# A neighbourhood-attention kernel whose start is re-ordered, whose TensorE runs dummy matmuls at the beginning, and whose first store moves to another queue

## The chip, the cores and the metric

One core of a Trainium2 chip. The metric is the time of the launch in device microseconds (us), taken over several runs; a trace is of one run, and its span is some 2 us shorter than that run's time. A run is called slow when it took over 1.5% longer than the fastest of the same kernel. The "clock" is the share of full speed that PE was granted, as the profile prints it. Engines: PE is TensorE (PEld its weight loads), DVE VectorE, ACT ScalarE, POOL GpSimd, SP the queue of SyncE. "L425" is line 425 of the kernel in question; a line has other numbers in the changed kernel.

## The reference

Dilated neighbourhood attention on a 224 x 224 image with 192 channels, one head, 7 x 7 neighbours at dilation 2, the window clipped at the borders:

```python
H = W = 224; C = 192; ks, dil = 7, 2
q, k, v = split(x @ wqkv)
r0 = clip(arange(H) - 6, 0, H - 1 - 12);  c0 = clip(arange(W) - 6, 0, W - 1 - 12)
ri = r0[:, None] + 2 * arange(7);         ci = c0[:, None] + 2 * arange(7)
logits = einsum(q, k[ri, ci]) * C ** -0.5            # 49 per pixel
o = einsum(softmax(logits), v[ri, ci]) @ wo
```

## The kernel before

Dilation 2 splits the image into even and odd rows and columns. The kernel works in 28 steps, numbered from 0: 14 row blocks j, each with two row classes rc. A step has 8 ticks; a tick takes one column class cc and three or four column tiles n. The query and key weights are folded into products AW, so that a "G" tensor (AW times x) is multiplied with x itself. Masks and one-hot keys ride along as extra rows of the contraction (the tiles called gbt and xb).

```python
for si, st in enumerate(steps):                   # 28 steps
    ...                                           # (cut) lists of work to slip in
    for ti, (cc, ns) in enumerate(st.od):         # 8 ticks
        G = s_stage(st, cc, ns)                   # scores: xa/ga and xb/gbt matmuls, exp on ACT
        if fill: fill.pop(0)()                    # (condition shortened) a G piece, or an output piece of the last step
        if prev is not None:
            y_stage(prev)                         # p (exp of scores) times x rows: needs the xn loads
            ...                                   # y_evac: two evictions, ACT and DVE
        if ti > 0:
            for f in pool_q[:2]: f()              # loads of x rows from POOL, key copies
            n_sp = 4 if st.rc == 0 else 1
            run(sp_q[:n_sp])                      # loads of x rows from SP
        if ti == 1 and st.rc == 0:
            load_xt(st.j + 2)                     # transposed block by DMA, on SP
```

`store` writes a step's output near the end of the following step. A usual step has 5 transfers. The two border steps have each row apart, 16 or so, and before the change all 16 of step 0 went through SP. Before step 0 the start loads 28 pieces of x, turns them on PE (84 transposes), makes the AW products and all of the first G kinds 0 and 1. Step 0's `first_fill` makes the rest, and all five further mask rows:

```python
def f4():
    for gi in range(1, NG):
        mask_row(gi)                              # DVE, 5 of them
    fill_groups(1)
    spread_keys(...); spread_cols(...); spread_rows(nc.sync, 1, NG); ...
    run(k01); run(p11); run(k11)                  # key copies, 7 loads on POOL, key copies
```

The softmax here doesn't subtract the row's maximum and nothing guards it: scores larger than these inputs give would overflow.

## Time and profile before

| | before |
|---|---|
| median time | 373.3 us (371.11 to 375.67, 15 runs) |
| span of the trace | 370.4 us |
| first scores / start of step 1 / step 2 / step 3 | 21.99 / 42.84 / 54.27 / 72.21 us |
| PE busy, share of the span | 336.4 us, 91% |
| PE idle on a DMA at the y matmuls | 6.0 us, 2 times |

Two stretches of 5 us show more:

```profile
35.00:40.00 5.00, 2.49 (x28) 1.83 (x29) 2.37 (x6) 1.68 (x4) 2.90 (x8) 0.58 1.08 207
40.00:45.00 5.00, 5.00 (x56) 3.51 (x54) 1.88 (x4) 3.40 (x8) 4.88 (x12) 0.74 0.60 131
```

After a pause of PE that ends at 37.51 the clock was 0.50 until 42.64, with PE busy for all of these 5.1 us.

### The profile page before, as it was taken

The numbers are of one execution on the slowest core, as the hardware profiler recorded it, in microseconds if no ns is written. First come the engines' busy times: TensorE is split into PE (matmuls) and PEld (weight loads), VectorE is DVE, ScalarE is ACT, GpSimd is POOL, SyncE is SP. The second block draws the span as 40 slices with busy tenths as digits, with TensorE's granted clock in tenths as the row PEclk, the third lists the DMA queues.
The fourth block names the chain that finished last, engine by engine and source line by source line (L and its number), as shares of the span: only waits on it lengthen the run. The fifth ranks groups of instructions, "written<-read, shape, count | busy, mean of one in ns | idle before, by whom it ended". The sixth has DMA issues, their size and how long they took to land.

```text
span 370.4 us, 12803 instructions
## 1 busy us (share of the span) xinstructions
PE 336.4 (91%) x5012; PEld 284.0 (77%) x5012; DVE 276.7 (75%) x692; ACT 238.9 (64%) x540; POOL 237.2 (64%) x481
## 2 busy tenths in 40 slices
PE   5876996799999999999899999999999999999990
PEld 2644685688888888788788888888888888888880
DVE  2779376487877877878787787877778888778791
ACT  4544674467677677776676767677676776677651
POOL 9639737168767697657966778667697649972002
PEclk9999699899999999999999999999999999999996
DMA  5849714676978659579695765957869586553233
GB/s 142 195 97 216 147 22 112 137 183 157 187 205 194 169 156 254 135 105 234 167 238 151 190 179 154 256 128 180 182 162 261 131 195 162 158 128 95 58 96 78
DMA packets 101808, 59.24 MB, mean 160 GB/s; under 512 B 83936, under 2 KB 96232, under 8 KB 101747
## 3 DMA queue, kind: packets, MB, share of 16 engines
q1 hardware_dynamic: 89315, 45.59, 52.7%
q0 software_dynamic: 11888, 12.29, 13.4%
q8 instruction: 39, 0.64, 0.7%
q10 hardware_dynamic: 544, 0.54, 0.6%
q14 instruction: 22, 0.18, 0.2%
HBM read 19.56 MB, written 19.27 MB: 105 GB/s over the span
## 4 chain that ended last, share of the span: by engine, by line
PE 58%; DVE 24%; SPq 5%; ACT 5%; DMA 3%; issue 2%; POOL 0%; POOLq 0%; DVEq 0%
PE pg L341 17%; PE y L425 14%; PE po L443 11%; DVE ysb L439 8%; PE s_ps L397 7%; PE s_ps L398 7%; DVE o_all L456 5%; DVE gbt L347 4%; ACT gbt L348 4%; SPq L504 3%; DMA xn<-in_x_dram 2%; SPq L86 2%; PE pe L307 2%; DVE gbt L236 2%; DVE xb L279 1%
## 5 line engine op out<-in xcount | busy, mean ns | idle before, releaser
L86 POOL DMA_DIRECT2D xn<-in_x_dram x245 | 136.5, 587 | 79.1 <-PE y L425 69.9
L402 ACT ACTIVATE p_sb<-s_ps 128x448 bf16<-128x448 f32 (+1 forms) x224 | 107.2, 490 | 33.4 <-PE s_ps L398 31.7
L425 PE MATMUL y<-p_sb,xn 128*128 128x112 bf16 (+3 forms) x1736 | 113.6, 207 | 6.0 <-DMA xn<-in_x_dram 6.0
L425 PEld LDWEIGHTS <-xn 128*128 128x128 bf16 (+1 forms) x1736 | 98.7, 98 | 23.1 <-DMA xn<-in_x_dram 6.3
L456 DVE TENSOR_TENSOR o_all<-po,rs 128x384 bf16<-128x384 f32 x189 | 105.3, 557 | 8.7 <-DVE rs L455 0.7
L341 PE MATMUL pg<-xt,aw 128*128 128x436 bf16 (+2 forms) x588 | 105.9, 299 | 4.2 <-DVE gbt L348 1.6
L397 PE MATMUL s_ps<-ga,xa 128*128 128x112 bf16 (+3 forms) x812 | 103.3, 211 | 0.6 <-ACT ga L344 0.6
L443 PE MATMUL po<-WP,ysb 128*128 128x193 bf16 x784 | 100.5, 249 | 3.5 <-ACT gbt L348 2.1
L398 PE MATMUL s_ps<-gbt,xb 128*128 128x112 bf16 (+3 forms) x812 | 102.0, 211 | 0.0
L439 DVE CAST ysb<-y 128x448 bf16<-128x448 f32 x104 | 64.6, 622 | 27.7 <-PE y L425 24.5
L397 PEld LDWEIGHTS <-xa 128*128 128x128 bf16 (+1 forms) x812 | 78.1, 99 | 5.4 <-issue 2.1
L398 PEld LDWEIGHTS <-xb 128*128 128x128 bf16 (+1 forms) x812 | 78.2, 99 | 3.5 <-issue 0.6
L443 PEld LDWEIGHTS <-ysb 128*128 128x128 bf16 x784 | 59.3, 98 | 8.6 <-issue 4.0
L439 ACT CAST ysb<-y 128x448 bf16<-128x448 f32 x104 | 57.6, 554 | 6.4 <-PE y L425 6.3
L341 PEld LDWEIGHTS <-aw 128*128 128x128 bf16 x588 | 42.6, 100 | 20.2 <-DVE o_all L456 6.1
L348 ACT CAST gbt<-pg 64x424 bf16<-64x424 f32 x54 | 27.4, 508 | 44.3 <-DVE gbt L347 44.3
L275 POOL COPY xa<-xt 128x896 bf16<-128x896 bf16 x56 | 53.0, 996 | 0.0
L455 DVE RECIPROCAL rs<-po 128x2 f32<-128x2 f32 x189 | 31.0, 164 | 27.5 <-PE po L443 25.6
L344 ACT CAST ga<-pg 128x436 bf16<-128x436 f32 x56 | 29.7, 530 | 26.3 <-PE pg L341 26.3
L347 DVE CAST gbt<-pg 64x436 bf16<-64x436 f32 x54 | 32.4, 599 | 3.9 <-PE pg L341 3.8
L365 POOL COPY ga<-ge 128x24 bf16<-128x24 bf16 (+5 forms) x60 | 20.9, 357 | 15.5 <-DVE ge L315 9.7
L350 ACT CAST ga<-pg 128x424 bf16<-128x424 f32 x56 | 28.7, 512 | 1.3 <-PE pg L341 1.2
(66 smaller groups left out, 152.3 us busy)
## 6 DMA issues: line engine op xcount, KB each, us to landing
out_dram<-o_all SPq DMA_DIRECT2D x26, 630.0 KB
xn<-in_x_dram POOLq DMA_DIRECT2D x245, 48.0 KB, 4.1
xn<-in_x_dram SPq DMA_DIRECT2D x147, 48.0 KB
out_dram<-o_all SPq DMA_DIRECT2D x11, 78.8 KB
gbt<-gbt SPq DMA_DIRECT2D x3, 280.0 KB
out_dram<-o_all SPq DMA_DIRECT2D x52, 9.0 KB
xb<-xb SPq DMA_DIRECT2D x3, 224.0 KB
out_dram<-o_all SPq DMA_DIRECT2D x26, 18.0 KB
```

Source lines behind the costliest of these rows:

```text
L86: eng.dma_start(out=XN[rc][p0:p0 + 64, XP * n + 128:XP * (n + 1)], in_=xp[r0: r0 + 15: 2, TW * n: TW * (n + 1), :])
L275: nc.gpsimd.tensor_copy(out=XA[:, cc, rc, :, q].rearrange("p n (r c) -> p r n c", c=TW), in_=t[:, 2 * cc, rc:16:2, :].rearrange("p r (n c) ...
L341: nc.tensor.matmul(pg[:, a_ - ra:b_ - ra, p0:p0 + S - 3], lhsT=AW[w], rhs=xt[b][:, k, la:lb:2, p0:p0 + S - 3], start=(i == 0), stop=(i == ...
L347: e0(out=Bt[0][0:64, ra:rb, 3:S], in_=pg[0:64, :, 0:S - 3])
L348: e1(out=Bt[1][64:128, ra:rb, 6:S], in_=pg[64:128, :, 3:S - 3])
L397: nc.tensor.matmul(o, lhsT=XA[:, cc, st.rc, n, G.kp], rhs=A[cc][:, :, a:b], start=True, stop=False)
L398: nc.tensor.matmul(o, lhsT=XB[:, cc, st.rc, n, G.kp], rhs=Bt[cc][:, :, a:b], start=False, stop=True)
L402: nc.scalar.activation(out=G.p[G.kp, 0:off], in_=s_ps[G.kp, 0:off], func=ACTF.Exp)
L425: nc.tensor.matmul(ys[kt][:, :, a_ - h0:b_ - h0], lhsT=xn[G.kp, l0:l0 + 128], rhs=pv[:, :, a_ - a:b_ - a], start=not ys[2 + kt], stop=True ...
L439: eng(out=dst, in_=src.rearrange("p r i t -> p t i r"))
L443: nc.tensor.matmul(po, lhsT=st.ysb[cc][:, kt, t, :], rhs=WP[:, cc, kt, :], start=(kt == 0), stop=(kt == 1))
L456: nc.vector.tensor_tensor(out=st.o[:, t], in0=po[:, :, 0:C], in1=rs[:].to_broadcast([128, 2, C]), op=ALU.mult)
```

## The change

The intent is to fill PE's idle places at the start. In four parts:

1. The right half of x (column tiles 7 to 13) is loaded and turned first; scores start as soon as its half of G is there, and the left half is turned inside step 0. 13 of the AW pieces become copies on POOL.
2. Dummy matmuls on zeros are to keep PE's clock up: 12 and 2 before the transposes, one behind each group of seven transposes, one a tick in step 0, four small ones behind each score group of step 0.
3. The border store of step 0 gets an output tile of its own and goes out on POOL, one transfer at the end of a step. In odd steps SP is given two loads a tick, not one.
4. Mask rows 3 to 5 are made in steps 1 to 3 instead of step 0.

The core of the diff (cut: the order of loads, the halves of the key copies and one-hots, the list of what step 0 does in which tick):

```diff
-    run(xn_items(0, 0, nc.sync))
-    run(xn_items(1, 0, nc.gpsimd))
-    load_xt(1)
+    first_n = list(range(NT // 2, NT)) + list(range(NT // 2))
+    x00, x10 = xn_items(0, 0, nc.sync), [xn_items(1, 0, e) for e in (nc.scalar, nc.gpsimd, nc.sync)]
+    run(x10[0][n] for n in first_n[:2]); run(x00[n] for n in first_n); run(x10[2][n] for n in first_n[11:])
+    def warm(n_):
+        t = ps_go.tile([128, 512], F32, name="warm", tag="go")
+        for i in range(n_):
+            nc.tensor.matmul(t[:], lhsT=zero[:, 0:128], rhs=zero[:], start=True, stop=True)
...
+    def edge_weights():                           # 13 pieces
+            nc.gpsimd.tensor_copy(out=AW[dst][...], in_=AW[src][...])
...
+    turn_x(1)                                     # right half; left half: turn_x(0) in step 0
+    late = [g_half(1, 1)]
+    g_half(0, 1)
+    edge_weights()
...
+            if st.border and not last:
+                edge_q.append(lambda dst=dst, src=src: nc.gpsimd.dma_start(out=dst, in_=src))
+        run(edge_q[:1]); del edge_q[:1]           # at the end of each step
...
-                n_sp = 4 if st.rc == 0 else 1
+                n_sp = 4 if st.rc == 0 else 2
...
+            if 0 < si < NG - 2 and ti == 5:
+                mask_row(si + 2)
+                spread_rows(nc.sync, si + 2, si + 3)
```

## The prediction

> **What bounds the kernel now.** I read the page first, for its two PE rows, then the busy time by stretch with the stretches cut at the step starts, then the start-up and two idle places of PE instruction by instruction, and last the queue of SP, because the longest idle place ends on a transfer.
>
> ```profile
> PE 336.4 (91%) x5012; PEld 284.0 (77%) x5012; DVE 276.7 (75%) x692; ACT 238.9 (64%) x540; POOL 237.2 (64%) x481
> PE   5876996799999999999899999999999999999990
> ```
>
> Of 370.4 us PE is busy 336.4. The tenths show where it is not: the first eight or so slices (0 to 70 us) and the last. In between it is full, so nothing in the middle can pay unless it takes PE work away, and this change takes none away.
>
> The kernel has 28 steps with 29 first-half score matmuls (L397) each, so every 29th of them in the trace starts a step: 21.99, 42.84, 54.27, 72.21, 83.50, 95.24, ... The busy time by stretch, cut there (columns: stretch, length, busy us and count of PE, PEld, DVE, ACT, POOL, then PE clock, DMA share, GB/s):
>
> ```profile
> 21.99:42.84 20.85, 17.09 (x178) 11.21 (x178) 14.79 (x26) 9.76 (x26) 16.55 (x32) 0.84 0.93 180
> 42.84:54.27 11.43, 11.22 (x171) 9.62 (x169) 8.36 (x22) 8.25 (x19) 5.18 (x11) 1.00 0.11 25
> 54.27:72.21 17.94, 12.64 (x185) 10.80 (x183) 9.23 (x24) 8.26 (x19) 8.42 (x16) 0.90 0.45 106
> 72.21:83.50 11.29, 11.08 (x173) 9.57 (x171) 9.27 (x23) 8.13 (x19) 8.08 (x16) 1.00 0.81 199
> 291.46:303.20 11.74, 11.50 (x186) 9.92 (x183) 8.99 (x24) 8.15 (x19) 8.43 (x16) 1.00 0.70 170
> ```
>
> Odd steps take 11.3 us and even ones 11.7, with PE 98% busy. Step 0 takes 20.85, step 2 takes 17.94. So there are three sums to win: what lies before 21.99 (no scores yet), the excess of step 0, and 17.94 - 11.69 = 6.25 us in step 2.
>
> The step 2 excess is one wait, seen in PE's and SP's timelines:
>
> ```profile
> 61.79 0.36 PE L425 MATMUL y<-p_sb,xn 128*128 128x112 bf16 x4
> 67.21 0.29 PE L425 MATMUL y<-p_sb,xn 128*128 128x64 bf16 x2 [5.06 <-DMA xn<-in_x_dram]
> ...
> 36.48 3.40 SPq L86 DMA_DIRECT2D xn<-in_x_dram  x5
> 53.80 11.03 SPq L504 DMA_DIRECT2D out_dram<-o_all  x16
> 64.88 3.51 SPq L86 DMA_DIRECT2D xn<-in_x_dram  x5
> ```
>
> SP is given six loads of x rows in step 1. Five go out at 36.48, and the sixth stands behind the store of border step 0, which is 16 small transfers, starts only when the outputs are done (53.8) and holds the queue 11.03 us. The load leaves at 64.88, and PE idles 5.06 us for it. The other 1.2 us is the slow clock after the pause.
>
> Step 0 is long for two reasons, in DVE's and POOL's timelines:
>
> ```profile
> 25.78 5.12 DVE L236 CAST gbt<-rm 32x896 bf16<-32x896 f32 x5
> 30.94 0.70 DVE L262 COPY xn<-grp 128x896 bf16<-128x896 bf16 x2
> 31.63 3.59 DVE L279 COPY xb<-xt 64x896 bf16<-64x896 bf16 x4
> 35.25 1.16 DVE L436 CAST ysb<-y 128x448 bf16<-128x448 f32 x2
> ...
> 29.82 4.15 POOL L86 DMA_DIRECT2D xn<-in_x_dram  x7
> 33.91 2.10 POOL L275 COPY xa<-xt 128x896 bf16<-128x896 bf16 x2
> 35.96 0.82 POOL L298 COPY xe<-xt 128x144 bf16<-128x144 bf16 x2
> ```
>
> DVE is without a gap from 25.8 to 36.9, and the evictions that PE needs (y, then the kind-1 G piece) stand behind five mask rows; PE idles 3.8 us, until 37.51. POOL meanwhile reaches the edge gather of block 1, which PE needs for the next step, at 35.96, too.
>
> **What the Trainium skill says.** "TensorE: Matmul & The Clock Gate", Part 1: The HAM clock gate, has PE at half rate until about 3.4 us of sustained matmuls and again after an idle window. The trace agrees: 128x112 score matmuls start 0.09 us apart at 22 us and 0.05 apart at 26 us, and the clock is 0.90 in the stretch with the 5 us pause. The dummy matmuls of the change are for this. "DMA: Bandwidth & Descriptors", Issuing engines are not separate DMA queues: spreading issues over engines saves only the sequencer's time to initiate. That time is just what counts here: 14 loads hold SP 9.16 us (0.65 each), 16 stores 11.03. "SBUF — State Buffer", Who interferes with whom: DVE copies in a two-port mode and GpSimd lock each other out. The trace fits: the key copy of L279 took 0.38 us at 19.42 and about 1.06 at 33, beside POOL's copies.
>
> **The change, part by part.** (1) Before step 0. Now 28 loads are awaited, all 84 transposes done, and all of the first G made, before scores at 21.99. The change loads and turns the right half first and makes only its half of G kinds 0 and 1. Its right-half loads are 7 on SP (after one weight load: 0.75 + 0.6 + 7 x 0.65 = 5.9), 2 on ACT, 5 on POOL after some 1.7 us of iotas (3.0 + 5 x 0.6 = 6.0). With 3.4 us from issue to landing (the DMA view's median before 16 us) they are in at 9.4. PE first runs 12 dummies of 512 columns: about 0.43 us each at the half rate (0.09 per 112 columns), 5 us or a little less, to 6.5. Then 8 weight transposes, their copies, now on two engines, and the AW products, whose copies drop from 17 to 8 because 13 pieces go later to POOL: to about 9.0. 42 transposes at 0.056 (36 took 2.1 us) plus 6 dummies of 0.21 are 3.7: 12.7. A copy 0.39, six G matmuls 0.6, ACT's eviction of the second G piece 0.5, small gaps: scores at 14.4, that is 7.6 earlier. Masks and one-hots lie beside the loads on an idle DVE.
>
> (2) Step 0. It takes on the left half: 42 transposes with six evictions of 0.39 to 0.53 (15.0 to 19.2), then gathering edges on POOL 0.9, G halves 1.0, the edge product, which must wait for a free PSUM buffer (21.2 to 21.8). The third score group then starts at about 21.8. Its seven followers each add scores 0.4, y 0.4, a dummy 0.2 and their share of G, WP and weight turns, 1.0 to 1.8 a tick: PE alone would reach step 1 at about 33. POOL is later: edges of block 0 are done at 24.4 (2.0 us as now), two half key copies 1.0, seven loads 4.15, two key copies 2.0 to 2.6, two more 2.1, gather 0.85: 34.5 to 35.1. PE runs the block 1 edge product 0.6 and two G pieces 0.9 after that: step 1 at about 36.2 instead of 42.84. That is 6.6 us. Of the 7.6 won at the front, 1.0 is given back. DVE has about 15 us of work in these 22, after three of five mask rows (3.1 us) are moved out.
>
> (3) The border store goes to POOL, one transfer at the end of each of 16 steps, from a tile of its own, and in odd steps SP gets two loads a tick, so all six leave before any store. This removes the wait of step 2 whole: 6.25 us. On POOL, 16 issues of about 0.6 us in steps where it is 74% busy (8.4 of 11.5) should be hidden.
>
> (4) Given back: mask rows of 1.02 us fall into steps 1, 2, 3, where DVE has 2.5 us free per step but evictions stand behind them; I charge 1.0 in all.
>
> Sum: 6.6 + 6.25 - 1.0 = 11.9. 373.2 - 11.9 = 361.3; I say 361.
>
> **The rivals.** A, *the front only moves*: the first scores come early, but step 0 swells to 26 us or more, because transposes, edge weights and key copies are pushed into it, so step 1 starts at 40 to 42 and only the step 2 wait is won. For it: POOL is already 16.55 of 20.85 busy in step 0 and gets 13 more copies (which I put at about 0.2 each from the 0.22 to 0.34 of its small edge copies) before it. Against: those lie mostly before the scores, and the moved mask rows free DVE. Time: 365 to 367. B, *the wait of step 2 is taken over*: the load is on time, but POOL's stores or the late load of block 2 (now issued at the end of step 0, some 6 us of SP) hold up what step 2 needs. For it: SP has about 17 us of issues to make between 15 and 32. Against: the six loads then leave by 42 and are needed at 50. Time: 363 to 366. C, *POOL is not the end of step 0*: its loads and copies start earlier than I have them, and PE's own work sets step 1 at 32 to 33. Time: 357 to 358. D, *all hidden already*: not credible, since the idle is on PE, which is full everywhere else.
>
> **Range and chances.** Rivals C and A give 357 and 367; with the scatter of the runs (371.97 to 375.67) the eight-in-ten range is 356.5 to 366. Faster by over 2% means under 365.8: it needs 7.5 of 11.9 us, and the step 2 wait alone is 6.25, so 0.90; within 2% 0.095; slower 0.005.
>
> **What would show it.** First scores near 14.4 (13.5 to 15.5), step 1 near 36 (33 to 38) with POOL's edge gather of block 1 just ahead of it, step 2 about 11.7 long without a DMA wait at its y matmuls, SP without a run of 16 stores, steps 1 to 3 longer than 11.3 and 11.7 by 1.0 together, steps from 5 on unchanged, half-rate matmuls gone after about 7 us. I am wrong if step 1 starts after 40, if step 2 keeps a wait over 2 us, or if later steps grow because of the stores on POOL.

## The result

The changed kernel takes 362.39 us (361.57 to 363.28, 10 runs) against 373.3. The ratio is 0.9705, 95% interval 0.9682 to 0.9728: 3.0% faster. A ratio here is the mean time of one kernel's fast runs over that of the other's of the same rounds, so not quite the ratio of the medians quoted beside it.

The page of the changed kernel, its first line of engines, the PE row, and the group of y matmuls:

```profile
PE 339.8 (94%) x5084; PEld 284.0 (79%) x5084; DVE 277.3 (77%) x702; ACT 236.4 (66%) x528; POOL 245.8 (68%) x507
...
PE   8999999999999999999999999999999999999980
...
L473 PE MATMUL y<-p_sb,xn 128*128 128x112 bf16 (+3 forms) x1736 | 112.3, 207 | 0.0
```

PE is now full from the second slice on, and in the last line the idle time before y matmuls, 6.0 us before, is 0.0. (Some of the busy time at the start is dummies.) Busy time by stretch, cut at the step starts, as before:

```profile
14.64:38.24 23.60, 22.15 (x276) 14.05 (x276) 15.79 (x35) 12.31 (x29) 13.80 (x30) 1.00 0.73 166
38.24:50.25 12.01, 11.51 (x171) 9.72 (x169) 8.70 (x22) 8.34 (x19) 8.76 (x19) 1.00 0.84 145
50.25:61.94 11.69, 11.45 (x185) 9.86 (x183) 9.94 (x27) 8.16 (x19) 9.59 (x18) 1.00 0.93 129
...
73.51:85.87 12.36, 11.63 (x186) 9.93 (x184) 10.13 (x28) 8.31 (x19) 9.39 (x18) 1.00 0.71 169
```

Set against the stretches of before, the two spans differ as follows (after minus before, us; step 3 is the stretch between the last two rows):

| before scores | step 0 | step 1 | step 2 | step 3 | step 4 | all later | sum |
|---|---|---|---|---|---|---|---|
| -7.35 | +2.75 | +0.58 | -6.25 | +0.28 | +0.62 | -0.23 | -9.60 |

So the time came from two places, the front (7.35, of which step 0 gives 2.75 back) and step 2. The queue of SP, and POOL's store, show step 2's side:

```profile
40.45 5.11 SPq L86 DMA_DIRECT2D xn<-in_x_dram  x6
...
50.45 2.72 SPq L86 DMA_DIRECT2D xn<-in_x_dram  x4
...
50.81 0.53 POOL L556 DMA_DIRECT2D out_dram<-o_all  x1 [3.57 <-DVE o_all L505]
```

All six loads leave SP from 40.45 on, ahead of any store, and POOL issues the first border transfer in 0.53 us. The end of step 0, POOL first and then PE:

```profile
33.76 1.22 POOL L327 COPY xe<-xt 128x144 bf16<-128x144 bf16 x2
...
35.52 0.54 PE L370 MATMUL pg<-xt,aw 128*128 128x109 bf16 x4 [0.72 <-ACT gbt L376]
35.99 0.54 PE L473 MATMUL y<-p_sb,xn 64*128 64x64 bf16 x10
36.46 0.39 PE L111 MATMUL warm<-zero 128*128 128x512 bf16 x1
36.81 0.47 PE L336 MATMUL pe<-xe,aw 128*128 128x48 bf16 x12
```

POOL has gathered the edges of block 1 at 34.98, but PE comes to their product only at 36.81. The trace therefore already speaks against POOL as the end of step 0, which was my step; In this stretch PE waits 0.72 us, until 35.52, for an eviction of DVE and ACT, and has no other wait that long. The experiments ask three things: is step 2's gain what I said it was and which of its two edits made it; what sets step 0; and what are the dummies and the moved mask rows worth.

### The profile page after: what moved, and what is told of

Read it like the earlier page. It is cut to its first block, busy times and chain, and to the rows that moved or that the text cites. A ratio compares the mean times of both kernels' runs of the same rounds, so it can differ in the third digit from the quotient of the medians.

```text
span 360.8 us, 12965 instructions
## 1 busy us (share of the span) xinstructions
PE 339.8 (94%) x5084; PEld 284.0 (79%) x5084; DVE 277.3 (77%) x702; ACT 236.4 (66%) x528; POOL 245.8 (68%) x507
## 4 chain that ended last, share of the span: by engine, by line
PE 63%; DVE 25%; ACT 6%; issue 3%; DMA 1%; POOL 0%; DVEq 0%; POOLq 0%; SPq 0%
PE pg L370 16%; PE y L473 13%; PE po L491 11%; DVE ysb L487 10%; PE s_ps L442 7%; PE s_ps L443 7%; DVE o_all L505 6%; DVE gbt L375 5%; ACT gbt L376 4%; PE warm L111 3%; PE pe L336 2%; DVE rs L504 1%; DVE xb L308 1%; DMA out_dram<-o_all 1%; PE tp_x L598 1%
## 5 line engine op out<-in xcount | busy, mean ns | idle before, releaser
L86 POOL DMA_DIRECT2D xn<-in_x_dram x240 | 134.1, 583 | 57.3 <-PE y L473 48.8
L450 ACT ACTIVATE p_sb<-s_ps 128x448 bf16<-128x448 f32 (+2 forms) x224 | 106.8, 489 | 35.0 <-PE s_ps L443 28.7
L473 PE MATMUL y<-p_sb,xn 128*128 128x112 bf16 (+3 forms) x1736 | 112.3, 207 | 0.0
L443 PE MATMUL s_ps<-gbt,xb 128*128 128x112 bf16 (+3 forms) x812 | 100.9, 210 | 0.2
L370 PE MATMUL pg<-xt,aw 128*128 128x436 bf16 (+2 forms) x567 | 97.9, 290 | 3.2 <-ACT gbt L376 0.7
L443 PEld LDWEIGHTS <-xb 128*128 128x128 bf16 (+1 forms) x812 | 77.3, 98 | 4.0 <-DVE gbt L391 0.6
L304 POOL COPY xa<-xt 128x896 bf16<-128x896 bf16 (+1 forms) x58 | 52.2, 948 | 2.6 <-ACT xt L599 2.6
L370 PEld LDWEIGHTS <-aw 128*128 128x128 bf16 x567 | 40.0, 98 | 17.4 <-DVE o_all L505 6.7
L373 ACT CAST ga<-pg 128x436 bf16<-128x436 f32 x54 | 28.5, 528 | 23.1 <-PE pg L370 23.1
```

Of the source, the lines that this page charges most:

```text
L86: eng.dma_start(out=XN[rc][p0:p0 + 64, XP * n + 128:XP * (n + 1)], in_=xp[r0: r0 + 15: 2, TW * n: TW * (n + 1), :])
L304: nc.gpsimd.tensor_copy(out=XA[:, cc, rc, n0:n1, q].rearrange("p n (r c) -> p r n c", c=TW), in_=xt[b][:, 2 * cc, rc:16:2, cols].rearrange ...
L370: nc.tensor.matmul(pg[:, a_ - ra:b_ - ra, p0:p0 + S - 3], lhsT=AW[w], rhs=xt[b][:, k, la:lb:2, p0:p0 + S - 3], start=(i == 0), stop=(i == ...
L443: nc.tensor.matmul(o, lhsT=XB[:, cc, st.rc, n, G.kp], rhs=Bt[cc][:, :, a:b], start=False, stop=True)
L450: nc.scalar.activation(out=G.p[G.kp, 0:off], in_=s_ps[G.kp, 0:off], func=ACTF.Exp)
L473: nc.tensor.matmul(ys[kt][:, :, a_ - h0:b_ - h0], lhsT=xn[G.kp, l0:l0 + 128], rhs=pv[:, :, a_ - a:b_ - a], start=not ys[2 + kt], stop=True ...
```

## The experiments

There were twelve runs of eleven kernels, all correct. The time of the kernel before in the same rounds was 373.4 to 374.0 us. In each, "A" is the changed kernel and "B" the kernel before.

| run | median us (all runs) | ratio to before (95% interval) |
|---|---|---|
| b_loads_first | 371.68 (369.34 to 376.99) | 0.9938 (0.9899 to 0.9977) |
| b_loads_first2, the same again | 376.43 (372.12 to 381.91) | 0.9967 (0.9932 to 1.0003) |
| b_store_pool | 368.16 (368.06 to 368.57) | 0.9867 (0.9840 to 0.9894) |
| a_undo_store | 369.89 (368.04 to 371.15) | 0.9907 (0.9872 to 0.9942) |
| a_loads_late | 364.56 (363.97 to 367.57) | 0.9781 (0.9749 to 0.9813) |
| a_no_dummy_step0 | 362.54 (358.02 to 367.59) | 0.9642 (0.9584 to 0.9699) |
| a_no_dummy | 363.53 (362.08 to 363.67) | 0.9698 (0.9659 to 0.9736) |
| a_mask_back | 365.40 (364.68 to 369.11) | 0.9777 (0.9726 to 0.9828) |
| a_mask_pool | 362.25 (361.97 to 362.83) | 0.9676 (0.9640 to 0.9713) |
| v_early | 362.06 (360.45 to 375.50) | 0.9687 (0.9663 to 0.9711) |
| v_early_few | 359.30 (358.32 to 359.65) | 0.9614 (0.9592 to 0.9637) |
| v_early_none | 364.03 (358.93 to 367.66) | 0.9710 (0.9660 to 0.9759) |

### The wait in step 2

**a_undo_store**: A with both edits of part 3 undone (the tile of its own stays).

```diff
-                n_sp = 4 if st.rc == 0 else 2
+                n_sp = 4 if st.rc == 0 else 1
...
-            if st.border and not last:
-                edge_q.append(lambda dst=dst, src=src: nc.gpsimd.dma_start(out=dst, in_=src))
-            else:
-                q.dma_start(out=dst, in_=src)
+            q.dma_start(out=dst, in_=src)
```

> The changed kernel with both edits to this queue undone: the border store back on SP in one burst and one load a tick in odd steps. What stays is the new start and the moved mask rows. Theory (the parts add up): step 2 gets its 6.2 us wait back, 368.5. Rival (with step 1 starting 4.6 us earlier the wait grows, because the load of block 2 is now issued just before the sixth load): 370 or more. If neither, and the time stays at 362 to 364, the wait was removed by something else.

```profile
50.97 10.12 SPq L555 DMA_DIRECT2D out_dram<-o_all  x16
61.14 3.55 SPq L86 DMA_DIRECT2D xn<-in_x_dram  x5
...
63.49 0.29 PE L473 MATMUL y<-p_sb,xn 128*128 128x64 bf16 x2 [4.92 <-DMA xn<-in_x_dram]
```

The wait is back with the same chain: 16 stores, the load behind them, 4.92 us of idle PE. Step 2 takes 18.67 us instead of 11.69, that is 6.98, and the median rises by 7.5. Part 3 is the step 2 gain, shown by undoing it.

**b_store_pool**: B with the store alone moved.

```diff
+            st.o = work.tile([...], tag="o_first" if first else "o_all", bufs=1 if first else 2)
...
+            if st.border and not last:
+                edge_q.append(lambda dst=dst, src=src: nc.gpsimd.dma_start(out=dst, in_=src))
...
+        run(edge_q[:1]); del edge_q[:1]
```

> The kernel before, with the border store of step 0 alone moved: a tile of its own, and one of its 16 transfers issued on POOL at the end of each step. Theory: the sixth load no longer stands behind 16 stores, step 2 falls to about 11.7 us, the time to about 367. Rival (POOL's stores hold up its key copies and loads): the wait goes, but later steps grow by 0.1 us each or more and the time stays above 369. If this and the run with the loads first both give the whole 6.2 us, either edit alone was enough.

Step 2 falls to 11.69 and the median by 5.3 us, not the whole 6.25. The trace has small waits of the same kind in later steps, the longest in step 24 (13.12 us long), SP and then PE:

```profile
311.78 4.34 SPq L510 DMA_DIRECT2D out_dram<-o_all  x5
316.23 3.40 SPq L86 DMA_DIRECT2D xn<-in_x_dram  x5
...
318.69 0.23 PE L425 MATMUL y<-p_sb,xn 128*128 128x64 bf16 x2 [1.51 <-DMA xn<-in_x_dram]
```

With one load a tick the sixth load of an odd step stands behind the ordinary store too, five transfers, and is at times late. (The kernel before had one of these too, 0.93 us in step 12.) A, which has the second edit as well, two loads a tick, shows 0.0 us idle in its row of y matmuls; no run adds that edit alone to this one.

**b_loads_first** and **b_loads_first2**: B with that second edit alone, run twice.

```diff
-                n_sp = 4 if st.rc == 0 else 1
+                n_sp = 4 if st.rc == 0 else 2
```

> The kernel before, with one number changed: in odd steps the SP queue gets two loads of x rows a tick instead of one, so the sixth load of step 1 is issued before the border store. Theory (the 5.06 us wait in step 2 is this one load behind 16 stores): step 2 falls from 17.9 to about 11.7 us with no DMA wait at its y matmuls, the time by 6.2 us to about 367. Rival (the 11 us of stores on SP are themselves the harm, since the loads and the transposed block of step 2 still follow them): step 2 or 3 keeps 2 us or more of the wait, 369 to 372.

> The kernel of the run with the loads first once more (two loads a tick in odd steps, nothing else), since that run's profile fell in the slow state and its four times lay between 369.3 and 377.0. In its (slow) profile step 2 was 11.7, but steps 4, 8 and 16 were 2 to 4 us too long. Theory (SP issues nearly all the time, so the 11 us burst of 16 stores, no longer absorbed by the pause, is repaid in later steps): a fast profile also shows step 2 near 11.7 and about 2 to 4 us of excess spread over later even steps, time 369.5 to 372. Rival (that was the slow state alone): a fast profile without such steps and 367.

The theory I had first, that this alone gives 6.2 us, is refuted: the fast runs of the two gain 0.6% and 0.3%, and the second interval reaches 1. Both profiles fell in the slow state (three of eight runs were slow), so I may not explain the loss from them. That SP has little slack, so that a burst of 16 stores which no pause absorbs is repaid later, is argued and not shown. What is shown: the loads first alone are worth 0.3 to 0.6%, the store moved alone 1.3%, and both together, undone in A, cost 7.5 us of 370.

### What sets the length of step 0

**a_loads_late**: A with seven loads of POOL moved behind its last edge copies, which frees POOL 4 us earlier.

```diff
-            run(p11[hn:])                         # in tick 2 of step 0
...
+            run(p11[hn:])                         # at the end of step 0
```

> The changed kernel with seven loads of x rows (4.0 us of issue on POOL) moved behind POOL's last edge copies of step 0, so that POOL reaches the edge gather of block 1 some 4 us earlier. My prediction said POOL's chain sets the start of step 1: then step 1 starts 1.5 to 2 us earlier than 38.2 and the time is about 360.5. The trace of the changed kernel says it is PE (busy 22.15 of 23.6 us in step 0, and at the edge product 1.8 us after the gather is done): then step 1 starts at 38.2 as before and the time is 362.4, within 0.3.

POOL, then PE, at the end of step 0; then DVE, POOL and PE at the end of step 1:

```profile
30.08 0.99 POOL L327 COPY xe<-xt 128x144 bf16<-128x144 bf16 x2
...
36.58 0.47 PE L336 MATMUL pe<-xe,aw 128*128 128x48 bf16 x12
...
48.48 2.33 DVE L308 COPY xb<-xt 64x896 bf16<-64x896 bf16 x1
...
48.34 1.83 POOL L304 COPY xa<-xt 128x896 bf16<-128x896 bf16 x2
...
50.87 0.22 PE L443 MATMUL s_ps<-gbt,xb 128*128 128x112 bf16 x1 [0.62 <-DVE xb L308]
```

POOL is done with the gather at 31.07 instead of 34.98, and PE comes to the edge product at 36.58 instead of 36.81; step 1 starts at 38.02 instead of 38.24 (its first scores came 0.28 later, so step 0 itself is 0.5 shorter). Of the 3.9 us by which POOL is earlier at most 0.5 comes through: POOL does not set it, and my step is refuted. The kernel is 2 us slower for another reason: POOL's key copies now fall beside DVE's, one of which takes 2.33 us where the copy of the same place takes 0.38 in A, and step 2 begins with waits and is 13.74 us long. (That POOL's copies hold up DVE's is read from their times; no run here takes them apart.)

**a_mask_back**: A with mask rows 3 to 5 again in step 0.

```diff
-            mask_row(2)
-            spread_rows(nc.sync, 2, 3)
+            for gi in range(2, NG):
+                mask_row(gi)
+            spread_rows(nc.sync, 2, NG)
...
-            if 0 < si < NG - 2 and ti == 5:
-                mask_row(si + 2)
-                spread_rows(nc.sync, si + 2, si + 3)
```

> The changed kernel with mask rows 3 to 5 put back into step 0 (behind the row of step 2, with one copy for all to the other partitions). My prediction charged the moved rows 1.0 us in steps 1 to 3; the traces show steps 1 to 4 longer by 1.5 in all than the same steps of the kernel before (without its wait). Theory (the rows cost more where DVE is without a gap, in step 0): steps 1 to 4 shrink by 1 to 1.5, step 0 grows by 1.5 to 3, time 362.5 to 364.5. Rival (in step 0 they fit DVE's gaps, PE sets it): step 0 unchanged, time 361.

DVE, then PE:

```profile
32.47 3.42 DVE L261 CAST gbt<-rm 32x896 bf16<-32x896 f32 x4
35.92 0.60 DVE L375 CAST gbt<-pg 64x436 bf16<-64x436 f32 x1
...
37.11 0.54 PE L370 MATMUL pg<-xt,aw 128*128 128x109 bf16 x4 [2.84 <-ACT gbt L376]
```

The eviction of a G piece stands behind four rows on DVE, PE waits 2.84 us instead of 0.72, and step 0 takes 26.36 instead of 23.60. The median is 3.0 us higher: that is what part 4 earns. It also divides the gain at the front: step 1 starts at 42.84 in the kernel before, at 40.48 here and at 38.24 in A, so of the 4.6 us some 2.2 belong to part 4 and 2.4 to parts 1 and 2 together (no run takes part 1 away by itself). Steps 1 to 4 did not get shorter (12.40, 11.69, 12.08, 11.75), against the other half of the expectation. But this trace can't settle what the rows cost there: its clock was 0.50 from 38.78 to 42.19, which reaches 1.7 us into step 1 (clock 0.93), and up to half of that may be lost time.

**a_mask_pool**: A with the mask rows of steps 1 to 3 on POOL.

```diff
-                mask_row(si + 2)
+                gk_ = gorder[si + 2]
+                nc.gpsimd.tensor_copy(out=GB[gk_ + (0,)][rsl], in_=rm[rsl, si + 2, :].unsqueeze(2).to_broadcast([32, BR, S]))
```

> The changed kernel with the mask rows of steps 1 to 3 written by POOL instead of DVE. Theory (the rows delay PSUM evictions on DVE, which PE waits for): steps 1, 3 and 4 lose their excess of 0.3 to 0.6 each, time 361. Rival (POOL's write locks DVE out of its copies, or POOL's other work in odd steps is late): no gain or 0.5 to 1 us slower.

No change in time (362.25): step 1 stays at 12.01, steps 3 and 4 take 12.39 and 11.75 instead of 11.57 and 12.36. The excess of steps 1 to 4, 1.5 us together, does not hang on which engine writes the rows. The traces narrow it down. Step 4's 0.6 is not there in four later traces with the same rows (11.74 or 11.75). Step 1's 0.6 is there in three of them as in this run (12.01 to 12.04; the fourth had a clock of 0.90 there), and 0.3 of it comes right at its start: the first `gbt` matmul begins 0.35 us after the first score matmul instead of 0.05, when DVE has just evicted the last G piece (38.48), long before step 1 makes its own mask row. The cause of the rest stays open.

### The dummies

**a_no_dummy_step0**: A without the dummies of step 0.

```diff
-                warm(1)                           # left half's transposes only
...
-                if si == 0:
-                    warm(1)
...
-        if st is steps[0]:
-            for i in range(4):
-                nc.tensor.matmul(s_ps[:, 448:512], lhsT=zero[:, 0:128], rhs=zero[:, 0:64], start=True, stop=True)
```

> The changed kernel without the dummy matmuls of step 0: the six of 512 columns between the left half's transposes, one a tick, and four of 64 columns behind each score group. Those at the start and in the right half's transposes stay. Theory A (PE sets the length of step 0, so its dummies cost their time): 13 at about 0.21 us and 32 at about 0.03, 3.7 us less PE work, the clock holds at full through the real work, step 1 starts 2 to 3.5 us earlier than 38.2, time 359 to 360.5. Theory B (the dummies hold the clock: transposes and short groups do not): half-rate matmuls come back for several us in step 0, step 1 starts at 38 or later, time 362 to 365.

Both happen. Two fast runs take 358.0 and 359.0 with a mean clock of 0.985, three take 362.5 to 363.2 with 0.976 to 0.977 (the sixth run, 367.59, is slow). The profile is of the second kind; busy time by stretch:

```profile
14.94:20.00 5.06, 3.95 (x73) 3.17 (x72) 3.23 (x10) 3.36 (x8) 1.64 (x5) 1.00 0.68 141
20.00:25.00 5.00, 5.00 (x55) 3.62 (x54) 2.37 (x9) 2.71 (x6) 3.79 (x13) 0.66 0.95 209
...
34.00:38.00 4.00, 3.90 (x37) 2.56 (x36) 1.93 (x5) 1.86 (x5) 0.94 (x4) 0.50 0.99 190
```

After five us with 42 transposes among 73 matmuls the clock (third column from the right) is 0.66, and after a wait of 2.57 us on DVE's backlog near 34 it is 0.50. The changed kernel has 1.00 in all of step 0. Its ratio (0.9705) is still no better than this run's 0.9642; the intervals overlap.

**a_no_dummy**: A without any dummy.

```diff
-    warm(12)
-    warm(2)
-                warm(1)                           # and all of the run above
```

> The changed kernel without any dummy matmul. Theory (PE at half rate until it has been busy for some us): weight products, transposes and first scores run at half rate, matmuls of 112 columns 0.09 us apart up to about 20 us or later. The weight turns start at 3 instead of 6 us, but x is not there before about 9, so first scores come at 14 to 15.5, not earlier than 14.6 by more than 1; step 0 is longer than without its dummies alone by 1 to 3 us; time 361 to 365. Rival (the clock matters little since other engines set the pace): as the run without step 0's dummies within 0.5 us.

```profile
25.00:30.00 5.00, 5.00 (x41) 3.33 (x39) 3.46 (x5) 2.94 (x9) 5.00 (x9) 1.00 0.74 177
```

PE gets through 41 matmuls in these five us, and A, some dummies among them, through 66; score matmuls of 112 columns are 0.09 us apart still at 30 us. Step 0 is 25.77 us long. First scores come at 13.91, which is no gain that can be told: traces of runs with all dummies at the start have them at 13.9 to 15.1. The span is 1.0 us longer than A's, and the ratios, 0.9698 and 0.9705, are not to be told apart. As placed in A, the dummies together earn about 1 us at most: they save half-rate time and cost PE time.

**v_early**: A with DVE's backlog moved into its idle places.

```diff
             onehot_keys(1)
+            mask_rows(slice(1, NG)); mask_row(1); mask_row(2)     # were in ticks 2, 3 and 4 (three lines in one)
...
-            fill_groups(1)                                        # was in tick 4
...
-                if h == 1 and (rc, k) in ((0, 1), (1, 0)):
-                    fill_groups(0, 1 + rc)
+                if (rc, k) in ((0, 1), (1, 0)):
+                    fill_groups(1 - h, 1 + rc)
```

> The changed kernel with DVE's backlog of step 0 moved: mask rows 1 and 2 right behind the second one-hot (DVE idle for 1.5 us there) and the group columns of the second x tile between the left half's transposes. All dummies stay. Theory (PE and DVE are about level in step 0, DVE costs PE only the 0.72 us wait at 35.5): step 1 starts 0.5 to 1 us earlier, time 361.5. Rival (PE alone sets it, or the moved work delays the transposes' evictions): no change, 362.4 within 0.4.

Five fast runs at 360.45 to 362.1, two slow ones at 369 and 375 with clocks of 0.966 and 0.939; the profile is a slow one. The median of the fast ones, 362.0, is within 0.4 us of A's: that DVE's wait alone is worth 0.5 to 1 us is not shown. The slow trace bears on the dummies, though, which are all in this kernel:

```profile
20.00:30.00 10.00, 9.28 (x77) 5.75 (x77) 4.35 (x15) 2.23 (x5) 1.62 (x6) 0.50 0.78 181
```

The clock fell to 0.50 at 10.97, among transposes with a dummy behind each seven, and stayed there until 31.45. The runs don't say why.

**v_early_few**: the same, and without the dummy a tick (seven, not eight as the expectation has it) and those behind the score groups. The dummies between transposes and at the start stay.

```diff
-                if si == 0:
-                    warm(1)
...
-        if st is steps[0]:
-            for i in range(4):
-                nc.tensor.matmul(s_ps[:, 448:512], ...)
```

> As the run with DVE's work early, and without the one dummy a tick and the four behind each score group; the dummies between transposes and at the start stay. Theory (with no DVE backlog PE is busy with counted matmuls without a pause after the transposes, so the clock holds): 8 x 0.2 + 32 x 0.03 = 2.6 us less PE work in step 0, time 359 to 360, all runs within 1 us. Rival (the clock falls as it did in the run without the dummies of step 0, clock 0.66 at 20 to 25 us): scatter of several us and a median of 361 to 363.

```profile
14.21:34.49 20.28, 18.74 (x237) 12.50 (x237) 12.80 (x35) 12.33 (x29) 13.31 (x31) 1.00 0.85 178
```

359.30 us, all five runs within 1.4 us, clock 1.00 in the whole of step 0. PE is busy 18.74 us in it where A has 22.15, and step 0 takes 20.28 where A takes 23.60: the work taken off PE is the time won. Against v_early, which differs by these dummies alone, the median of the fast runs falls by 2.7 us. This version beats both kernels; 3.9% faster than before, ratio 0.9614.

**v_early_none**: the same without any dummy in step 0.

```diff
-                warm(1)                           # left half's transposes too
+                if h == 1:
+                    warm(1)
```

> As the run with DVE's work early, with no dummy in step 0 at all. Theory (a run of transposes lets the clock fall: in the run without step 0's dummies it was 0.66 right after them): the clock drops after the left half's transposes in some or all runs, scatter of 3 us or more, median 360 to 363. Rival (only the DVE pause at 34 made it fall): steady, 358.5.

```profile
15.00:20.00 5.00, 3.51 (x48) 2.44 (x43) 3.96 (x13) 2.12 (x5) 1.57 (x3) 0.75 0.81 166
20.00:25.00 5.00, 4.28 (x44) 3.01 (x42) 2.15 (x9) 2.45 (x5) 2.75 (x11) 0.56 0.88 200
```

Among its fast runs one takes 358.93 us at a mean clock of 0.983 and three 363.9 to 364.1 at 0.966 to 0.970. The other two, 364.5 and 367.66, are slow. The profile is of the run at 358.93; no trace shows one at 364. The clock falls after the transposes (0.75, then 0.56). The two kernels differ by the six dummies between the left half's transposes: with them all five runs have a mean clock of 0.99, without them all six have 0.983 or less. So in this order of work these six hold the clock and the ones on the ticks only cost time. Two limits: in v_early the mean clock was 0.966 and 0.939 in two of seven runs with all dummies in place, so they are no guarantee; and the dummies also fill pauses (PE is busy 3.51 us of 15 to 20 here and 5.00 in A), so no run says whether it is the transposes or the pauses beside them that lose the clock.

## Why the prediction was right, and where not

The time, 361.0 predicted and 362.4 measured, and the range held. Its terms:

- **Before step 0: right.** 14.4 predicted, 14.64 measured; the gain 7.6 and 7.35.
- **Step 2: right, and shown by undoing it.** 6.25 predicted, 6.25 in the profile; 6.98 when part 3 is taken out of A. I had given both edits one effect. The runs show that each has a share: the store moved alone gives 5.3 us, the loads first alone 0.3 to 0.6%.
- **Step 0: the size nearly, the cause wrong.** "PE alone would reach step 1 at about 33. POOL is later" is the step that failed. POOL's gather was done at 34.98, inside my 34.5 to 35.1, and freeing POOL 4 us earlier moved step 1 by 0.2 us. The mis-sized term is PE's work in step 0: I left out the four small dummies behind each of eight score groups and put the rest of the ticks too low. PE was busy 22.15 us there, and step 1 came at 38.24, not 36.2. The term of 6.6 us was 4.6. The sum had a second fault that partly hid the first: after the third score group it counts seven more, but step 0 has eight groups, so five follow. From the third group (22.48) to step 1 six ticks took 15.76 us, 2.6 each, where "1.0 to 1.8 a tick" was put; the two faults partly cancel, and that its 33 was not further off is luck. Rival C, that PE ends step 0, was right in its mechanism and wrong in its direction.
- **Mask rows: the charge was of about the right size, and its reason is not shown.** I charged 1.0 for rows in steps 1 to 3; these steps are 0.86 longer (steps 1 to 4 1.5), but the excess did not leave when POOL wrote the rows, and part of step 1's comes before its row is made. What part 4 earns, 3.0 us, had no term of its own in the sum: it is inside that of step 0.
- **The dummies: taken for granted.** I counted those between the transposes and on the ticks at 0.2 us each, but never asked whether they pay. Those between the transposes do; the ones on the ticks and behind the score groups cost most of 3.3 us, and the best version comes from leaving them out. The account of step 0 before names DVE and POOL and puts no price on the clock: 5.1 us of work at 0.50 there are, as an estimate, 2.6 us lost. A keeps 1.00 in step 0 and pays for it with dummies.

Of 2.3 us too much in the sum of the profile (11.9 against 9.6), 2.0 are step 0's end. That the medians came nearer (10.9) is luck: the profiled run of the kernel before was one of its faster ones.

## What to carry to other kernels

A transfer that PE needs soon should never stand in an in-order queue behind stores that wait for the end of a step: look at the queue's own timeline, and move both, the burst to a queue with slack and the load ahead of it. When a phase looks limited by one engine, add up the others' work to the same precision, with the helper instructions that the change itself adds; here the second busiest engine by my count was the first. In this kernel dummy matmuls paid where the clock would fall, among transposes, and not where real matmuls kept a clock that was already up (those of a_no_dummy still ran at the half rate at 30 us): take each group out by itself, and look at the clock of every run.

## What the Trainium skill lacked or had wrong

- "TensorE: Matmul & The Clock Gate", Part 4: PE-mode transpose, says that the full clock "doesn't engage" for transposes. The runs agree and add that a clock that was up can be lost behind a run of transposes: 0.66 and 0.56 between 20 and 25 us, after 42 of them, against 1.00 with one 512-column dummy behind each seven (but 0.50 in one slow trace with these dummies). That page does not say what such a dummy buys.
- The same page, Part 1, says that the number of slow matmuls at the start varies from run to run, and calls this ramp less than 1% of a typical span. It gives no figure for a clock that is lost again after the start. Here, without dummies among the left half's transposes, fast runs of one kernel lie at 359 or at 364 us, 1.4% apart, with the clock at 0.983 or 0.967.
- Its caveat on clock events ("Seeing it yourself", in the same part) has no word on the time before the first event: without dummies the profile prints a clock of 1.00 over step 0 while matmuls of 112 columns start 0.09 us apart, twice the 0.05 of the full rate. The spacing is the thing to read.
- "DMA: Bandwidth & Descriptors", Issuing engines are not separate DMA queues, calls the issue time "usually small relative to the DMA itself". For one transfer the runs agree: 0.65 us on SP for a 48 KB load, and 3.4 from issue to landing for one of the same size on POOL. It has no word on the sum in one queue: 16 small stores held SP for 11.03 us, and PE waited 5.06 us for the load behind them.
- "SBUF — State Buffer", Who interferes with whom, has the loser of the shared port blocked for the other's whole instruction. The page has no case of several in a row: a DVE copy that takes 0.38 us in A took 2.33 beside two POOL copies one behind the other, and ended after both (50.81 against 50.17).
